# Attention with hashed buckets and a feed-forward block on one core: five kept heads instead of six, GpSimd instructions in column pieces, another order

## The chip, the cores and the metric

The kernel runs on one core of a Trainium2 chip. The metric is the device time in microseconds (us) of one execution; three runs of the kernel before gave a median of 906.74 us. The core's engines are called as in the profile: PE (TensorE, matrix products), DVE (VectorE), ACT (ScalarE), POOL (GpSimd) and SP (SyncE, which issues most DMAs).

## What is computed

Four batches, eight heads, 768 positions, 64 values a head. Queries and keys get a bucket from the signs of six random projections; a position attends only to keys of its own bucket. The attention's output is then put through a feed-forward block with a gelu between two products.

```python
q_bits = (np.einsum('bhsd,dk->bhsk', q, proj) > 0)      # the same for k
mask = q_bucket[:, :, :, None] == k_bucket[:, :, None, :]
scores = np.where(mask, scale * np.matmul(q, k.transpose(0, 1, 3, 2)), -1e9)
attn = exp(scores - max); attn = attn / (attn.sum(-1) + 1e-9)
attn_out = np.matmul(attn, v)                           # (4, 8, 768, 64)
x = attn_out.transpose(0, 2, 1, 3).reshape(3072, 512)
h = x @ w_in                                            # 512 -> 2048
out = (0.5 * h * (1.0 + erf(h / sqrt(2)))) @ w_out      # 2048 -> 512
```

## The kernel before

**Attention.** A unit is 128 query rows of one head against all 768 keys; there are 192 of them. In a unit PE makes the scores (`scores`, L940 in float32, L942 and L943 in half precision), DVE takes the largest of each row out of PSUM (L946), a guard and a shift are worked out for each row (L951 and the helper `affine`, L427 on DVE and POOL, L424 on ACT), ACT takes the exponentials (L960), and DVE the reciprocal of the row sums (L969). Then the probabilities are turned over: for early units by PE transposes (L1019) that DVE or ACT copy out of PSUM into `pt`, later as a rounded half and the rest of it (L427 or L424, and L975) by a DMA transpose. PE multiplies them by the values (L1063 in float32, L1072 in halves).

**Heads.** A head's queries and keys lie in a set of buffers, and the mask is put into extra rows of these. `head_plain` builds a set in float32: two loads, a projection on PE (L893), a sign on ACT, four mask copies. `head` builds it in half precision, each value as a rounded number and a remainder: a load (L588), the largest value on DVE (L591), a scale over all rows (L548 on PE, four small DVE steps), the rounding, three moves of rows, two remainders (L622 on DVE, or on POOL a scaling by L427 and a subtract by L447), a projection (L656), a sign (L662) and four mask copies. Scores of a plain head are two float32 products a unit, of the other heads four half-precision ones.

**Passes.** Batch 0 is worked in two passes over its heads: first 256 query positions (two units a head), then the other 512 (four units a head). Batches 1 to 3 take one pass each. All eight heads of the first pass are plain (`PLAIN = (8, 0)`). Sets with a number below `AGAIN` stay for the second pass, and their heads are used there as they are; the others are built anew by `head`.

**Weights.** The two weight matrices are read as 64-bit words and decoded on DVE (L713, L718, L723), their scale comes from products on PE (L736), and each pair is scaled, rounded and its remainder taken (L427, L424, L447) on ACT, DVE or POOL. This goes on during batch 0. The first product with the output weights waits for all of it.

**Feed-forward.** For each 256 positions PE multiplies by the input weights (L1288), ACT empties PSUM (L1298) and takes the gelu (L1326), the result is split into two halves (L427 or L424, and L1340 on DVE), and PE multiplies by the output weights (L1370). DVE applies the scales (L1400), SP stores.

**Order.** Nothing is ordered by hand. Every step is given to `Plan.add` with a key (what comes first), the steps it needs, a buffer of a ring, and the engines that can do it, each with a cost and an offset. `Plan.order` plays the program through once while it is built: whenever an engine is free, it takes the ready step with the lowest key plus offset. The offsets and many leads in the keys are the numbers in `PAR`, such as `GU_Pool` (the guard on POOL) or `QK1` (scores of the second pass). In that play-through a POOL step and a DVE step marked `port=True` hold a common resource for their whole cost. The result is a fixed order of instructions on each engine. `BLANKS` adds 64 steps of four small products whose results nobody reads, with a late key.

**What the change touches.** `affine` (L419 to L427) and `subtract` (L445 to L447) issue one instruction each for a whole tile. POOL's tiles are up to 1024 columns wide.

Of the kernel before, what the change touches and what calls it, by code (L numbers as in the profile page):

```python
# [16 lines left out]
ALU = mybir.AluOpType  # L17
# [7 lines left out]
FIRST = (((0, 256),), ((256, 256), (512, 256)))  # L25
NEARLY = 2
PLAIN = (8, 0)
AGAIN = 6
BARE = False
WHOLE = (4, 4, 0, 0, 0)  # L30
TABLE = 1.3
# [3 lines left out]
GROW = ("p","hl")  # L35

PAR = dict(
    VB=-40.97, GU_DVE=240.54, GU_Pool=100.45, SH_DVE=167.52, SH_ACT=204, SH_Pool=-19.66, SF_DVE=464.07,
    SF_ACT=-187.68, SF_Pool=-31.21, SU=12.36, NM_DVE=-98.7, NM_ACT=56.76, NM_Pool=-320.58, NM_SP=-162.08,
    NL_DVE=-344.19, NL_Pool=-241.09, XP_ACT=-25.57, XP_DVE=-138.99, NK_DVE=-194.15, NK_ACT=144.23, NK_Pool=21.84,  # L40
    Z=92.38, VS0=-8.93, H0=143.65, HL=-860.3, VS=-892.69, G2=312.6, HQ=577.2, VQ=-429.05, in0=-158.71, out0=424.19,
    in1=-31.4, out1=-40.75, in2=-97.83, out2=-238.27, in3=-146.98, out3=-601.69, H1=-55.7, H2=43.97, H3=-141.96,
    H4=210.7, H5=-617.14, H6=-992.69, H7=-275.83, MEV=-86.92, MGE=-79.83, MSP=-13.76, V0=-31.49, QK0=-585.17,
    QK1=13.9, QK2=-33.94, MX0=267.65, MX1=6.62, MX2=22.49, EX0=-389.34, EX1=-216.58, EX2=102.74, NR0=-69.88,
    NR1=62.63, NR2=328.32, HI0=-23.58, HI1=344.52, HI2=3.95, LO0=119.76, LO1=-21.28, LO2=-1288.81, PV0=-156.22,
    PV1=6.13, PV2=-3.3, TR0=507.72, TR1=-1210.58, TR2=10.73, V1=-212.82, V2=-786.36, Sin0=131.94, Sin1=-52.34,
    Sin2=912.32, Sin3=370.61, Sout0=-163.67, Sout1=81.17, Sout2=33.28, Sout3=700.51, Lin=-140.4, Pin=325.04,
    Qin=957.5, Cin=717.18, Min=-39.13, Lout=-10.95, Pout=-180.7, Qout=-1494.55, Cout=84.08, Mout=-22.24, G0=11.13,
    G1=-61.72, G3=7.9, G4=-238.53, G5=-133.32, G6=227.56, G7=-48.68, DUP0=258.78, DUP1=70.51, DUP2=148.98,
    LOW0=-28.06, LOW1=-108.23, LOW2=151.28, PRJ0=-266.56, PRJ1=451.66, PRJ2=57.45, MSK0=-121.55, MSK1=141.13,  # L50
    MSK2=-103.38, DI_ACT=-220.12, DI_DVE=456.39, DI_Pool=18.53, WS_ACT=839.42, WS_DVE=327.31, WS_Pool=297.28,
    WH_ACT=-283.58, WH_DVE=-111.37, WH_Pool=25.64, WL_ACT=169.18, WL_DVE=120.19, WL_Pool=-197.71, VH_ACT=-176.14,
    VH_DVE=-223.29, VH_Pool=414.86, RND_ACT=472.43, RND_DVE=132.9, RND_Pool=-47.28, HI_ACT=172.21, HI_DVE=-121.04,
    HI_Pool=-46.69, DG_ACT=-163.33, DG_DVE=110.27, DG_Pool=-117.55, EV_ACT=30.92, EV_DVE=1834.91, EV_Pool=-39.8,
    GH_ACT=-198.96, GH_DVE=138.26, GH_Pool=76.2, NS0=116.81, NS1=-68.13, NS2=-261.86,
)
FULL = 65504.0
BIG = 2.0**34
# [18 lines left out]
class Plan:  # L77
# [25 lines left out]
    def add(self, engine, cost, emit, key, needs=(), takes=None, table=None, port=False, act=1.0):  # L103
        s = Step(len(self.steps), engine, cost, emit, key, needs, takes, table, port, act)
        self.steps.append(s)
        return s
# [7 lines left out]
    def free(self, holder, after):  # L114
        hold = {"holder": holder, "left": len(after)}
        for s in after:
            s.frees.append(hold)
# [134 lines left out]
def tile_bucket_attention_moe(  # L252
# [94 lines left out]
    def buf(step):  # L347
# [32 lines left out]
        out=praw[:, NBIT:], in0=praw[:, :NBIT], scalar1=-1.0, scalar2=None, op0=ALU.mult  # L380
# [19 lines left out]
    def add_scale(key, top, t, inv, s, root=False):  # L400
# [17 lines left out]
            top = add("DVE", 0.07, emit, key, [top], port=emit is inverse)  # L418
        return top  # L419

    def affine(engine, out, in_, scale=1.0, bias=0.0):

        if engine == "ACT":
            nc.scalar.activation(out=out, in_=in_, func=AF.Copy, scale=scale, bias=bias)  # L424
        else:
            on = nc.vector if engine == "DVE" else nc.gpsimd
            on.tensor_scalar(out=out, in0=in_, scalar1=scale, scalar2=bias, op0=ALU.mult, op1=ALU.add)  # L427

    def affine_cost(engine, n, pointer=False):
        base, rate, extra = {  # L430
# [13 lines left out]

    def subtract(engine, out, in0, in1):  # L445
        on = nc.vector if engine == "DVE" else nc.gpsimd
        on.tensor_tensor(out=out, in0=in0, in1=in1, op=ALU.subtract)  # L447

    def subtract_cost(engine, n):
        return 0.14 + 1.042e-3 * n if engine == "DVE" else 0.2 + 2.2e-3 * n  # L450
# [4 lines left out]
    def everywhere(t, top, key):  # L455


        def diagonal():
            affine(dg.engine, buf(dg), ident, t[:, 0:1])

        def spread():
            nc.tensor.matmul(buf(pm)[:, :P], ones, buf(dg), start=True, stop=True)

        def biggest():
            nc.vector.tensor_reduce(out=t[:, 1:2], in_=buf(pm)[:, :P], axis=AX.X, op=ALU.max)

        dg = add(affine_on("DI", P, True), 0, diagonal, key, [top], takes="diag", port=True)
        pm = add("PE", 0.11, spread, key, [dg], takes="hp")
        free(dg, [pm])
        sc = add("DVE", 0.2, biggest, key, [pm])  # L470
        free(pm, [sc])
        return sc
# [105 lines left out]
    def head(b, h, i, key, clear, cl):  # L578
# [16 lines left out]
        def high():  # L595
            affine(hi.engine, aq, buf(raw), sc)

        def add_move(dst, src, rd, rs):
            box = []

            def move():
                out, in_ = sets[i][dst][rd], sets[i][src][rs]
                if box[0].engine == "SP":
                    nc.sync.dma_start(out=out, in_=in_)
                else:
                    affine(box[0].engine, out, in_)

            on = {
                "DVE": (0.27, PAR["NM_DVE"]), "ACT": (0.84, PAR["NM_ACT"]), "Pool": (0.9, PAR["NM_Pool"]),
                "SP": (0.45, PAR["NM_SP"]),  # L610
            }
            box.append(add(on, 0, move, key + PAR[f"DUP{cl}"], [hi], port=True))
            return box[0]

        def add_low(dst, rd, rs):
            box = []

            def low():
                out, a = sets[i][dst][rd], aq[rs]
                x = buf(raw)[rs]  # L620
                if box[0].engine == "DVE":
                    nc.vector.scalar_tensor_tensor(  # L622
                        out=out, in0=x, scalar=sc[rs], in1=a, op0=ALU.mult, op1=ALU.subtract
                    )
                else:
                    affine("Pool", x, x, sc[rs])
                    subtract("Pool", out, x, a)

            on = {"DVE": (1.04, PAR["NL_DVE"]), "Pool": (2.8, PAR["NL_Pool"])}
            box.append(add(on, 0, low, key + PAR[f"LOW{cl}"], [hi], port=True))  # L630
            return box[0]
# [160 lines left out]
    def v_scale(b, key):  # L792
# [16 lines left out]
        def load_rows(k):  # L809
            nc.sync.dma_start(  # L810
                out=v_first[:, 2 * k : 2 * k + 2], in_=v[b].rearrange("(c p) d -> p c d", p=P)[:, 2 * k : 2 * k + 2]
            )

        def biggest_rows(k):
            nc.vector.tensor_reduce(
                out=stat_v[:, b, k : k + 1], in_=v_first[:, 2 * k : 2 * k + 2], axis=AX.XY, op=ALU.max,
                apply_absolute_value=True,
            )

        parts = []  # L820
        for k in range(KT // 2 if b == 0 else 0):
            first_v.append(add("SP", 1.8, lambda k=k: load_rows(k), key))
            parts.append(add("DVE", 1.14, lambda k=k: biggest_rows(k), key + PAR["VB"], first_v[-1:]))
        for pr in range(NPAIR if b else 0):
# [10 lines left out]
        if b == 0:  # L835
            key += PAR["VB"]
            early_steps.extend(parts)
# [86 lines left out]
    def unit(t, i, qs, cl, whole, made, place, back):  # L924
# [70 lines left out]
        free(sp, [ex])  # L995
        on = {"DVE": (0.08, PAR["SF_DVE"]), "ACT": (0.23, PAR["SF_ACT"]), "Pool": (0.25, PAR["SF_Pool"])}
        sf = add(on, 0, safe, t - PAR[f"NR{cl}"], [ex])
# [137 lines left out]
    whole = tuple((c, TC) for c in range(0, S, TC))  # L1135
# [26 lines left out]
    for n_pass, (b, chunks) in enumerate(passes):  # L1162
# [7 lines left out]
        for pos, h in enumerate(heads):  # L1170
            pr = h // 2
            if pos % 2 == 0:
                key, mms = t - PAR[f"V{cl}"], []
                whole = pos // 2 < WHOLE[n_pass]
# [6 lines left out]
            i = next((i for i in range(n_sets) if owner.get(i, ())[:2] == (b, h)), None)  # L1181
            kept = i is not None
            if not kept:
                i = min(range(n_sets), key=lambda i: (used.get(i, -1), i))
# [29 lines left out]
        for i in list(owner):  # L1214
            if i >= AGAIN:
                del owner[i]
# [245 lines left out]
```

## Time and profile before

| | |
|---|---|
| three runs | 904.43, 906.74, 910.39 us |
| profiled execution | 905.23 us, span of its instructions 903.4 us |
| granted TensorE clock, mean | 0.991 |
| instructions | 18142 |
| busy ACT | 638.8 us (71%) x1098 |
| first and last product with the input weights (L1288) | 137.7 and 881.4 us |
| first and last product with the output weights (L1370) | 206.7 and 899.4 us |
| last row maximum of a unit (L946) | 725.7 us |

Rows of the profile that name a line and tiles, such as `L427 POOL TENSOR_SCALAR raw<-raw,hs`, give engine, operation, what is written and what is read. In the list of groups the numbers behind the bar are busy us, the mean ns of one instruction, and the idle us of the engine before it with what ended it. In the list of one line's instructions they are minimum, median and maximum in ns, and first and last start in us. In a timeline the first number is the start, the second the duration, both in us, and in brackets stands idle time before it and its releaser. In a table by stretches the stretch is followed by the busy us (and number of instructions) of PE, PE's weight loads, DVE, ACT and POOL, then the granted clock, the DMA share and GB/s. In a list of waits stand the sum in us, the number and the longest.

### The profile page before, as it was taken

Reading aid. Unit: us, or ns where it says so; the run is one execution under the profiler, and the core shown is the slowest. Engines: PE = TensorE matmul, PEld = TensorE weight load, DVE = VectorE, ACT = ScalarE, POOL = GpSimd, SP = SyncE. Lnnn points to the kernel's source line nnn. Section 1 sums busy time; section 2 is a strip of 40 time slices with the busy share of each in tenths; the row PEclk is TensorE's granted clock in tenths of the full one; section 3 lists DMA queues with packets and bytes.
Section 4 is the critical chain, followed back from the end, with each engine's and each line's share of the span. In section 5 each row is a group of like instructions: output and inputs, shape, how many; then the busy total and the mean of one; then the engine's idle time right before and its main releaser. Section 6 shows DMA issues by size and latency. Waiting matters only on the chain.

```text
span 903.4 us, 18142 instructions
## 1 busy us (share of the span) xinstructions
PE 870.2 (96%) x6883; PEld 581.0 (64%) x6883; DVE 686.4 (76%) x1402; ACT 638.8 (71%) x1098; POOL 434.5 (48%) x509
## 2 busy tenths in 40 slices
PE   8999889979999999999999999999999999999998
PEld 5666557756666666676757666757657667676663
DVE  3999989998988799889988998799877861212122
ACT  3687878988888997868998877798877653232221
POOL 2335546667587766766666667666534400000000
PEclk9999989999999999999999999999999999999999
DMA  9962543305597899685968976967767750000000
GB/s 215 241 215 72 146 134 103 106 1 93 97 187 156 163 178 213 123 158 139 174 138 191 190 134 147 177 130 152 134 112 133 134 112 1 24 1 24 1 24 24
DMA packets 281368, 110.67 MB, mean 123 GB/s; under 512 B 228608, under 2 KB 268992, under 8 KB 281280
## 3 DMA queue, kind: packets, MB, share of 16 engines
q1 hardware_dynamic: 280976, 109.51, 57.0%
q8 instruction: 54, 0.88, 0.4%
q14 instruction: 34, 0.28, 0.1%
q10 hardware_dynamic: 304, 0.00, 0.0%
HBM read 42.73 MB, written 6.29 MB: 54 GB/s over the span
## 4 chain that ended last, share of the span: by engine, by line
PE 48%; DVE 8%; ACT 6%; DMA 4%; issue 2%; POOL 1%; SPq 0%; ACTq 0%; POOLq 0%; DVEq 0%
PE hp L1370 19%; PE hp L1288 18%; PE hp L1072 4%; PE s L942 3%; DMA pt<-hl 3%; PE s L943 3%; DVE rows L946 2%; DVE hl L975 2%; ACT p L960 2%; DMA vraw<-v 1%; ACT Q L424 1%; ACT wraw L960 1%; DVE g L1340 1%; DVE wraw L975 1%; ACT hl L424 1%
## 5 line engine op out<-in xcount | busy, mean ns | idle before, releaser
L1288 PE MATMUL hp<-x,Win 128*128 128x256 f16 x2304 | 267.6, 273 | 0.6 <-DVE rows L427 0.3
L1370 PE MATMUL hp<-Wout,g 128*128 128x512 f16 x1152 | 261.5, 379 | 0.0
L1288 PEld LDWEIGHTS <-Win 128*128 128x128 f16 x2304 | 224.3, 98 | 40.2 <-issue 4.0
L1370 PEld LDWEIGHTS <-g 128*128 128x128 f16 x1152 | 110.2, 98 | 127.0 <-issue 5.1
L946 DVE TENSOR_REDUCE rows<-s 128x1 f32<-128x768 f32 x192 | 179.5, 947 | 8.5 <-PE s L943 4.6
L960 ACT ACTIVATE p<-s,rows 128x768 f32<-128x768 f32 x143 | 140.9, 986 | 22.7 <-DVE rows L427 7.7
L1298 ACT ACTIVATE h<-hp,ffs 128x512 f32<-128x512 f32 x96 | 65.3, 681 | 98.4 <-PE hp L1288 98.3
L942 PE MATMUL s<-Q 88*128 88x384 f16 x304 | 99.3, 327 | 8.8 <-ACT p L960 7.2
L427 DVE TENSOR_SCALAR g<-h,ffs 128x512 f16<-128x512 f32 x31 | 15.3, 497 | 111.0 <-ACT h L1326 80.9
L943 PE MATMUL s<-K 128*128 128x384 f16 x304 | 99.2, 326 | 0.0
L427 POOL TENSOR_SCALAR rows<-rows 128x1 f32<-128x1 f32 x111 | 48.6, 437 | 63.9 <-ACT p L960 41.9
L1340 DVE SCALAR_TENSOR_TENSOR g<-h,ffs,g 128x512 f16<-128x512 f32 x96 | 76.1, 806 | 2.8 <-DVE g L427 0.5
L1072 PE MATMUL hp<-pt,vhl 128*64 128x256 f16 x1296 | 76.5, 274 | 0.3 <-ACT h L1298 0.3
L1072 PEld LDWEIGHTS <-vhl 128*64 128x64 f16 x1296 | 68.6, 110 | 10.9 <-issue 10.4
L447 POOL TENSOR_TENSOR K<-raw,Q 64x768 f16<-64x768 f32 x42 | 72.7, 1730 | 3.5
L951 POOL TENSOR_SCALAR rows<-rows,hs 128x1 f32<-128x1 f32 x72 | 47.7, 662 | 51.1 <-DVE rows L946 44.0
L975 DVE SCALAR_TENSOR_TENSOR hl<-p,rows,hl 128x768 f16<-128x768 f32 x54 | 57.7, 1071 | 5.7 <-ACT hl L424 3.0
L960 ACT ACTIVATE wraw<-s,rows 128x768 f32<-128x768 f32 x49 | 48.3, 987 | 7.4 <-POOL rows L427 4.3
L943 PEld LDWEIGHTS <-K 128*128 128x128 f16 x304 | 29.8, 98 | 30.2 <-issue 14.0
L975 DVE SCALAR_TENSOR_TENSOR wraw<-p,rows,wraw 128x768 f16<-128x768 f32 x42 | 45.8, 1090 | 4.1 <-POOL wraw L427 4.0
L427 POOL TENSOR_SCALAR raw<-raw,hs 64x768 f32<-64x768 f32 x42 | 46.0, 1094 | 4.5 <-PE hp L1019 2.2
L940 PE MATMUL s<-K,Q 76*128 76x384 f32 x112 | 44.2, 527 | 3.7 <-ACT p L960 3.5
(163 smaller groups left out, 1371.0 us busy)
## 6 DMA issues: line engine op xcount, KB each, us to landing
raw<-qk SPq DMA_DIRECT2D x26, 384.0 KB, 3.6
vraw<-v SPq DMA_DIRECT2D x24, 384.0 KB, 4.0
wraw<-w_in SPq DMA_DIRECT2D x16, 512.0 KB, 4.6
wraw<-w_out SPq DMA_DIRECT2D x16, 512.0 KB, 4.1
out<-o SPq DMA_DIRECT2D x11, 512.0 KB, 2.8
K<-Q SPq DMA_DIRECT2D x24, 96.0 KB, 2.8
v_first<-v SPq DMA_DIRECT2D x3, 512.0 KB, 11.9
vhl<-v SPq DMA_DIRECT2D x4, 384.0 KB, 7.1
```

The source lines that it names most:

```text
L427: on.tensor_scalar(out=out, in0=in_, scalar1=scale, scalar2=bias, op0=ALU.mult, op1=ALU.add)
L447: on.tensor_tensor(out=out, in0=in0, in1=in1, op=ALU.subtract)
L942: nc.tensor.matmul(to, aq[kk, qs], ak[kk, n], start=True, stop=False)
L943: nc.tensor.matmul(to, bq[:, qs], bk[:, n], start=False, stop=True)
L946: nc.vector.tensor_reduce(out=nm, in_=both(sp), axis=AX.XY, op=ALU.max, negate=True)
L960: nc.scalar.activation(out=buf(ex).rearrange("p (b k) -> p b k", b=2), in_=both(sp), func=AF.Exp, scale=sc, bias=nb, accum_out=ssum,)
L975: nc.vector.scalar_tensor_tensor(out=buf(hi)[:, 1], in0=buf(ex), scalar=r, in1=buf(hi)[:, 0], op0=ALU.mult, op1=ALU.subtract,)
L1072: nc.tensor.matmul(pv[j * D : (j + 1) * D], buf(vh)[:, tv, kt, j * D : (j + 1) * D], buf(holds[j][0])[:, tp * KT + kt, :nt], start=kt == 0 ...
L1288: nc.tensor.matmul(buf(pair[0])[:, j * ch[1] : (j + 1) * ch[1]], win_hl[:, f0 // WB1, tw, pr, f0 % WB1 : f0 % WB1 + P], x[:, tx, pr, : ch[1]],
L1298: nc.scalar.activation(out=values_of()[:, 2 * fp : 2 * fp + 2, :nt], in_=buf(pair[0])[:, : 2 * nt].rearrange("p (j k) -> p j k", j=2), fun ...
L1340: nc.vector.scalar_tensor_tensor(out=gt[:, 1, s2, :nt], in0=h[:, s2, :nt], scalar=sg, in1=gt[:, 0, s2, :nt], op0=ALU.mult, op1=ALU.subtract,)
L1370: nc.tensor.matmul(buf(banks[u]).rearrange("p (c f) -> p c f", c=NWB), gt[:, tg, f, u * P : (u + 1) * P], wout_hl[:, :, tw, ft], start=ft ...
```

## The change

`AGAIN` goes from 6 to 5: five heads of batch 0 stay in float32 for its second pass, and three, not two, are built anew in half precision. `affine` and `subtract` cut a POOL instruction along the first axis behind the partitions when it has more than 512 or 256 elements a partition: 768 columns of a scaling become two instructions of 384, 768 of a subtract three of 256, 1024 two of 512 or four of 256. DVE and ACT instructions stay whole, and the costs that the plan counts with stay as they are. All numbers of `PAR` are other ones, so `Plan.order` gives another order and another division between engines.

```diff
-AGAIN = 6
+AGAIN = 5
...
 PAR = dict(
-    VB=-40.97, GU_DVE=240.54, GU_Pool=100.45, SH_DVE=167.52, SH_ACT=204, SH_Pool=-19.66, SF_DVE=464.07,
-    SF_ACT=-187.68, SF_Pool=-31.21, SU=12.36, NM_DVE=-98.7, NM_ACT=56.76, NM_Pool=-320.58, NM_SP=-162.08,
+    VB=67.25, GU_DVE=142.88, GU_Pool=372.81, SH_DVE=-85.93, SH_ACT=493.57, SH_Pool=68.35, SF_DVE=-887.75,
+    SF_ACT=162.31, SF_Pool=108.68, SU=-62.77, NM_DVE=132.71, NM_ACT=-36.16, NM_Pool=115.43, NM_SP=44.22,
...
+    def pieces(engine, most, *aps):
+
+        whole, n = aps[0].shape[1], 1
+        for size in aps[0].shape[1:]:
+            n *= size
+        count = -(-n // most) if engine == "Pool" else 1
+        cuts = [whole * k // count for k in range(count + 1)]
+        return [tuple(x[:, i:j] for x in aps) for i, j in zip(cuts, cuts[1:])]
...
     def affine(engine, out, in_, scale=1.0, bias=0.0):
...
             on = nc.vector if engine == "DVE" else nc.gpsimd
-            on.tensor_scalar(out=out, in0=in_, scalar1=scale, scalar2=bias, op0=ALU.mult, op1=ALU.add)
+            for o, x in pieces(engine, 512, out, in_):
+                on.tensor_scalar(out=o, in0=x, scalar1=scale, scalar2=bias, op0=ALU.mult, op1=ALU.add)
...
     def subtract(engine, out, in0, in1):
         on = nc.vector if engine == "DVE" else nc.gpsimd
-        on.tensor_tensor(out=out, in0=in0, in1=in1, op=ALU.subtract)
+        for o, x, y in pieces(engine, 256, out, in0, in1):
+            on.tensor_tensor(out=o, in0=x, in1=y, op=ALU.subtract)
```

The prediction speaks of the guard's offsets (`GU_`) and those of the step that adds 1e-9 (`SF_`); the other numbers of `PAR` change in the same way and are left out here.

More of the change, by code (lines that the diff above doesn't have):

```diff
@@ L37 @@
 PAR = dict(
-    VB=-40.97, GU_DVE=240.54, GU_Pool=100.45, SH_DVE=167.52, SH_ACT=204, SH_Pool=-19.66, SF_DVE=464.07,
-    SF_ACT=-187.68, SF_Pool=-31.21, SU=12.36, NM_DVE=-98.7, NM_ACT=56.76, NM_Pool=-320.58, NM_SP=-162.08,
-    NL_DVE=-344.19, NL_Pool=-241.09, XP_ACT=-25.57, XP_DVE=-138.99, NK_DVE=-194.15, NK_ACT=144.23, NK_Pool=21.84,
-    Z=92.38, VS0=-8.93, H0=143.65, HL=-860.3, VS=-892.69, G2=312.6, HQ=577.2, VQ=-429.05, in0=-158.71, out0=424.19,
-    in1=-31.4, out1=-40.75, in2=-97.83, out2=-238.27, in3=-146.98, out3=-601.69, H1=-55.7, H2=43.97, H3=-141.96,
@@ L43 @@
[L43 to L52, printed above, removed]
@@ L53 @@
-    VH_DVE=-223.29, VH_Pool=414.86, RND_ACT=472.43, RND_DVE=132.9, RND_Pool=-47.28, HI_ACT=172.21, HI_DVE=-121.04,
-    HI_Pool=-46.69, DG_ACT=-163.33, DG_DVE=110.27, DG_Pool=-117.55, EV_ACT=30.92, EV_DVE=1834.91, EV_Pool=-39.8,
-    GH_ACT=-198.96, GH_DVE=138.26, GH_Pool=76.2, NS0=116.81, NS1=-68.13, NS2=-261.86,
+    VB=67.25, GU_DVE=142.88, GU_Pool=372.81, SH_DVE=-85.93, SH_ACT=493.57, SH_Pool=68.35, SF_DVE=-887.75,
+    SF_ACT=162.31, SF_Pool=108.68, SU=-62.77, NM_DVE=132.71, NM_ACT=-36.16, NM_Pool=115.43, NM_SP=44.22,
@@ new lines @@
+    NL_DVE=-21.95, NL_Pool=-504.75, XP_ACT=-123.39, XP_DVE=180.18, NK_DVE=-90.24, NK_ACT=-257.23, NK_Pool=-55.95,
+    Z=-107.86, VS0=65.79, H0=-112.84, HL=-846.73, VS=-934.16, G2=389.39, HQ=129.83, VQ=-373.79, in0=-133.17,
+    out0=545.05, in1=-218.36, out1=37.81, in2=194.95, out2=21.39, in3=465.04, out3=52.59, H1=3.14, H2=-183.97,
+    H3=-155.9, H4=131.48, H5=-603.75, H6=-1004.23, H7=-195.76, MEV=266.52, MGE=696.78, MSP=15.46, V0=-120.7,
+    QK0=-118.82, QK1=-287.83, QK2=-180.25, MX0=-320.05, MX1=-49.19, MX2=-219.29, EX0=-612.78, EX1=-167.36,
@@ new lines @@
+    EX2=70.44, NR0=-89.58, NR1=33.83, NR2=-17.38, HI0=-561.14, HI1=248.83, HI2=340.6, LO0=106.64, LO1=-1263.75,
+    LO2=-161.71, PV0=99.03, PV1=115.36, PV2=-77.27, TR0=-1005.23, TR1=-480.94, TR2=45.98, V1=105.26, V2=-194.1,
+    Sin0=149.2, Sin1=64.71, Sin2=7.41, Sin3=246.53, Sout0=-231.58, Sout1=-272.11, Sout2=-372.59, Sout3=194.04,
+    Lin=-157, Pin=341.2, Qin=1120.37, Cin=100.83, Min=-140.12, Lout=-105.73, Pout=458.37, Qout=-2863.3,
+    Cout=-238.38, Mout=162.39, G0=-122.8, G1=-209.72, G3=488.78, G4=20.46, G5=-83.65, G6=-236.82, G7=27.83,
@@ new lines @@
+    DUP0=78.15, DUP1=-85.93, DUP2=-123.07, LOW0=-97.07, LOW1=-66.78, LOW2=18.58, PRJ0=-51.38, PRJ1=841.88,
+    PRJ2=-212.69, MSK0=-114.42, MSK1=426.71, MSK2=228.3, DI_ACT=138.03, DI_DVE=-27.21, DI_Pool=-60.85,
+    WS_ACT=419.32, WS_DVE=65.06, WS_Pool=-21.69, WH_ACT=-803.88, WH_DVE=7.52, WH_Pool=-245.54, WL_ACT=-154.68,
+    WL_DVE=-7.58, WL_Pool=72.47, VH_ACT=-163.46, VH_DVE=-112.9, VH_Pool=63.2, RND_ACT=86.42, RND_DVE=222.34,
+    RND_Pool=221.18, HI_ACT=230.76, HI_DVE=-182.55, HI_Pool=-59.39, DG_ACT=-153.24, DG_DVE=84.64, DG_Pool=151.66,
@@ L56 @@
+    EV_ACT=296.59, EV_DVE=1365.55, EV_Pool=34.42, GH_ACT=-144.99, GH_DVE=2.32, GH_Pool=-76.31, NS0=220.81,
+    NS1=-94.09, NS2=63.07,
 )
```

## The prediction

> **What bounds the kernel now.** I read the page's first part, then the busy times by stage, then what PE (TensorE) waited for.
>
> ```profile
> PE 870.2 (96%) x6883; PEld 581.0 (64%) x6883; DVE 686.4 (76%) x1402; ACT 638.8 (71%) x1098; POOL 434.5 (48%) x509
> ```
>
> ```profile
> 0.00:206.00 206.00, 185.63 (x1393) 125.16 (x1394) 181.87 (x423) 156.06 (x285) 104.14 (x139) 0.96 0.49 136
> 206.00:650.00 444.00, 435.53 (x3643) 289.99 (x3642) 396.19 (x795) 373.81 (x647) 301.94 (x329) 1.00 0.79 155
> 650.00:750.00 100.00, 99.22 (x844) 67.38 (x842) 74.58 (x132) 67.76 (x122) 28.40 (x42) 1.00 0.62 115
> ```
>
> The second fence gives, after the stretch, busy us of PE, PEld, DVE (VectorE), ACT (ScalarE) and POOL (GpSimd). I cut at 206 us because the first matmul against the output weights starts there. Behind it PE has feed-forward work to fill every hole: 435.5 of 444 us are busy, and 99.2 of 100. Ahead of it, PE is busy for 185.6 of 206 and DVE for 181.9: both are nearly full, and PE's 20.4 us of idleness there are 61% of the 33.2 us (903.4 - 870.2) it has in all. So the end moves in two ways: PE gets less work, or PE idles less. What DVE, ACT or POOL save counts only as far as PE was waiting for it.
>
> ```profile
> PE s L942 <- ACT p L960: 7.2, 13, 1.2
> PE hp L1063 <- DVE pt L427: 4.2, 3, 2.2
> PE s L940 <- ACT p L960: 3.9, 5, 1.4
> PE hp L736 <- DVE pt L427: 2.3, 1, 2.3
> ```
>
> PE's longest single waits (2.2, 2.3 us) are for DVE to empty a PSUM bank. They start elsewhere:
>
> ```profile
> 197.65 2.13 POOL L447 TENSOR_TENSOR Wout<-o,Wout 128x1024 f16<-128x1024 f32 x1
> 198.00 0.20 DVE L951 TENSOR_SCALAR rows<-rows,hs 128x1 f32<-128x1 f32 x1
> 198.12 2.21 DVE L427 TENSOR_SCALAR Wout<-o 128x1024 f16<-128x1024 f32 x1
> 198.13 0.19 PEld L1063 LDWEIGHTS hp<-pt,vhl 128*64 128x64 f32 x2 [2.03 <-DVE pt L427]
> 198.13 0.65 PE L1063 MATMUL hp<-pt,vhl 128*64 128x256 f32 x2 [1.80 <-DVE pt L427]
> ```
> ```profile
> 200.37 1.01 DVE L427 TENSOR_SCALAR pt<-hp 128x384 f32<-128x384 f32 x2
> ```
>
> A GpSimd subtract of 1024 columns runs from 197.65 to 199.78. DVE's scaling starts at 198.12 and ends only at 200.33, just after the subtract; behind it stand the two PSUM evictions of 200.37, and PE idles. The reader is to see the chain: long POOL instruction, stretched DVE instruction, late eviction, idle PE. That the stretch is a wait shows in a line whose instruction is always the same size:
>
> ```profile
> L713 DVE TENSOR_SCALAR Wout<-wraw x16: 402/420/2136, 96.2 to 180.7; 128x512 int32<-128x512 int32 x16
> ```
>
> Minimum, median and maximum are 402, 420 and 2136 ns.
>
> **Part 1: the column pieces.** Removed: one long hold of what DVE waits for. Added: more POOL instructions. The price of a cut comes from two widths of each form:
>
> ```profile
> L427 POOL TENSOR_SCALAR raw<-raw,hs x42: 892/907/1689, 90.6 to 648.2; 64x768 f32<-64x768 f32 x42
> ...
> L427 POOL TENSOR_SCALAR g<-h,ffs x18: 687/692/1837, 201.8 to 701.3; 128x512 f16<-128x512 f32 x18
> ...
> L447 POOL TENSOR_TENSOR K<-raw,Q x42: 1633/1640/2224, 92.1 to 649.2; 64x768 f16<-64x768 f32 x42
> ...
> L447 POOL TENSOR_TENSOR Win<-o,Win x8: 2122/2132/2314, 67.9 to 143.4; 128x1024 f16<-128x1024 f32 x8
> ```
>
> Scaling: (907 - 692)/256 = 0.84 ns a column, so 692 - 512 x 0.84 = 0.26 us does not depend on the columns, and each cut adds that. Subtract: (2132 - 1640)/256 = 1.92 ns, 0.17 us a cut; a 256-column piece is an estimated 0.66 us where the whole took 1.64 or 2.13. Fourteen groups of POOL scalings have 768 or 1024 columns, from the 42 above to 2 of the output weights:
>
> ```profile
> L427 POOL TENSOR_SCALAR Wout<-o 128x1024 f16<-128x1024 f32 x2 | 2.4, 1196 | 0.1
> L447 POOL TENSOR_TENSOR Wout<-o,Wout 128x1024 f16<-128x1024 f32 x4 | 9.7, 2430 | 0.4 <-ACT Wout L424 0.2
> ```
>
> They are 162 instructions, one cut each: 162 x 0.26 = 42 us. Subtracts: 42 x 2 cuts and (8 + 4) x 3, so 120 x 0.17 = 20 us. POOL gains 62 us of work; its queue is 48% busy and holds it, but 68% (302 of 444) from 206 to 650, where an estimated 45 of the 62 fall: 78%.
>
> What DVE gets back up to 206: the means of L713 for both weights stand beside its median of 420,
>
> ```profile
> L713 DVE TENSOR_SCALAR Win<-wraw 128x512 int32<-128x512 int32 x16 | 10.9, 686 | 1.1 <-DMA wraw<-w_in 1.1
> ...
> L713 DVE TENSOR_SCALAR Wout<-wraw 128x512 int32<-128x512 int32 x16 | 9.4, 595 | 0.7 <-DMA wraw<-w_out 0.6
> ```
>
> 16 x (0.686 + 0.595 - 2 x 0.42) = 7.1 us for this line. With the 1.7 us from 198.12 to the subtract's end at 199.78 and an estimated 6 for the decoding's other two lines (twice as many instructions as L713) and the rest, I take 15 us of waiting in this stage; a piece leaves a third of a wait on a subtract and some 60% of one on a scaling, so about 9 come back. The stage's DVE is 88% full and PE's waits for evictions above sum to 6.5 us, so I pass half on: **-4.5 us**. Bounds: 0, if PE waits for something else each time, and -9, if all of it counts. Beyond 206 DVE gains as much and POOL loses 45 us, and PE idles for only 8.5 us: I take -0.5, with -4 (half of that idleness) and +10 (the rival below) as bounds.
>
> **Part 2: five heads instead of six.** Head 5 of batch 0 is built a second time, in half precision. PE gives up 4 float32 score units and gets 4 half-precision ones, a projection and one scale:
>
> ```profile
> 157.96 2.85 PE L940 MATMUL s<-rest,x 76*128 76x384 f32 x8
> ```
> ```profile
> 194.80 0.33 PE L942 MATMUL s<-Q 88*128 88x384 f16 x1
> 194.96 0.33 PE L943 MATMUL s<-K 128*128 128x384 f16 x1
> ```
>
> A float32 unit is two calls, which the trace shows as four instructions; so this row is two units, and less the drain of the last one (0.2, an estimate) a unit costs 1.3 us. The half-precision matmuls follow each other every 0.165 us, four a unit: 0.66. So 4 x (1.3 - 0.66) = 2.6 us less, and 0.5 for the projection and 0.2 for the scale more:
>
> ```profile
> 125.10 0.51 PE L656 MATMUL hp<-K,hash 128*32 128x384 f16 x8
> ```
>
> **-1.9 us** of PE. DVE gets a largest-value reduction (0.95 us) and four small ones (an estimated 0.7):
>
> ```profile
> L591 DVE TENSOR_REDUCE tops<-raw 128x1 bf16<-128x768 f32 x26 | 24.6, 946 | 4.0 <-DMA raw<-qk 3.9
> ```
>
> At the same half, +0.8 us. The rounding, two low parts, the row moves and the masks go to whichever of ACT, POOL and DVE is free; if both low parts fall to DVE it is 2 us more, +1 on the path. The extra load (SP queue, one head, 384 KB) goes out well ahead, since set 5 is free after the first pass; if it came late, the head's projection and scores would wait and PE with them, since its order is fixed. Bounds of this part: -2 and +2.
>
> **Part 3: the order.** New offsets mean other neighbours for every instruction. They lean the small row steps towards DVE (guard: POOL 100 to 373, DVE 241 to 143; the 1e-9 step: DVE 464 to -888). A guard costs
>
> ```profile
> L951 DVE TENSOR_SCALAR rows<-rows,hs x80: 184/210/216, 171.7 to 727.5; 128x1 f32<-128x1 f32 x80
> L951 POOL TENSOR_SCALAR rows<-rows,hs x72: 292/710/1563, 175.3 to 720.8; 128x1 f32<-128x1 f32 x72
> ```
>
> 0.21 us on DVE and 0.71 on POOL, so exponentials start earlier and DVE gets up to 72 x 0.21 = 15 us. That PE waits 7.2 + 3.9 us for exponentials says how much there is to win, about 11; DVE's 15 at half say what there is to lose, 7.5. I take -1.5, between them.
>
> Sum: -4.5 - 0.5 - 1.9 + 0.8 - 1.5 = -7.6 us. The profiled execution took 905.2 us (span 903.4 and 1.8 around it), so 897.6. The median of the three runs is 906.7, 1.5 above it; I leave 0.9 for that: **898.5 us**.
>
> **The rivals.**
> *POOL becomes the bound between 206 and 650 (slower).* Its busy time grows by 45 us for cuts, and each of some 200 pieces there can wait for a DVE instruction: the 42 scalings of raw average 1094 ns against a median of 907, 0.19 a time, so 38 us more. 302 + 45 + 38 = 385 of 444, 87%, and some stretches over 100%. From that point guards and masks stand behind pieces, exponentials come late, and PE, whose order is fixed, waits: 1 us more at each of the 13 waits of L942 is +13, and 905.2 + 13 - 1.9 + 1.5 is **918**. For it: POOL guards already take 0.71 instead of 0.29. Against: PE idles 2% there, and lighter DVE makes up part of it.
> *The pieces run into each other and DVE gets nothing back.* Then only the 62 us of POOL and -1.9 remain: +3 on the path, **908**. The Trainium skill (GPSIMD Engine Reference, 2.1 Instruction dispatch) says that a GpSimd core starts the next instruction as soon as its own share of this one is done, and that nothing else holds consecutive instructions apart; by that rule the hold need not end between pieces. Against it stands a case of two POOL instructions back to back:
>
> ```profile
> 644.95 0.90 POOL L427 TENSOR_SCALAR raw<-raw,hs 64x768 f32<-64x768 f32 x1
> ...
> 645.09 1.56 DVE L975 SCALAR_TENSOR_TENSOR hl<-wraw,rows,hl 128x768 f16<-128x768 f32 x1
> ...
> 645.93 2.22 POOL L447 TENSOR_TENSOR K<-raw,Q 64x768 f16<-64x768 f32 x1
> ```
>
> The DVE instruction, stretched to 1.56, ended at 646.65, and the subtract took 2.22 instead of 1.64: DVE got in between the two.
> *The relief is real but PE's waits only change their name*, as PE is at 98% after 206: **905.5**.
> *The order closes most of the early idleness:* three quarters of the 20.4 us (15.3), half of the 8.5 behind it (4.2) and part 2's 1.1: 905.2 - 20.6 + 0.9 = **885.5**. For it: PE also spends 21.1 us on blank matmuls that only keep it running, so the early stage has more room than its idleness tells. Against: DVE, 88% full there, has to do its work in less time.
>
> ```profile
> L392 PE MATMUL hp<-blank 128*128 128x128 bf16 x256 | 21.1, 249 | 3.5 <-DVE both_offs L506 1.9 <-DVE hash L375 1.0 <-ACT pt L424 0.6
> ```
>
> **How the numbers follow.** This kernel's runs tell about 1% from no change, which is 9.1 us of 906.7. Forecast 0.50, of which 0.20 below 897.7 and 0.30 above; POOL bound 0.16, of which 0.14 over 915.8; no gap between pieces 0.06, 0.02 of it over that line; waits renamed 0.10; better order 0.18. Faster by over 1%: 0.20 + 0.18 = 0.38. Slower: 0.14 + 0.02 = 0.16. Within: 0.46. The range runs from 883, just under the better order, to 917, just short of the POOL rival; the forecast's own is 890 to 907.
>
> **What would show it.** Right: L713 and the other stretched DVE lines average near their medians (L713 below 0.5 us); POOL busy rises by 50 to 100 us with some 280 more instructions; L940 has 16 instructions fewer and L591 counts 27; the first output matmul starts 3 to 8 us before 206; PE busy falls by about 2 us plus what the filler matmuls lose. Wrong: the first output matmul no earlier than 206; DVE lines as stretched as before; or PE's idleness between 206 and 650 above 15 us with POOL as the releaser.

## The result and the profile after

Four runs of the changed kernel: 916.18 to 919.17 us, median 916.68, beside 907.47 for the kernel before. The ratio is 1.0107, with a 95% interval of 1.0069 to 1.0146: about 1% slower, where 1% faster was forecast. The profiled execution took 916.96 us, its span is 915.1. Two single executions of other runs below, 1218 and 1471 us at granted clocks of 0.68 and 0.56, are left out of all medians.

The first part of the page of the changed kernel:

```profile
PE 865.3 (95%) x6893; PEld 574.4 (63%) x6893; DVE 677.9 (74%) x1441; ACT 648.7 (71%) x1090; POOL 484.9 (53%) x745
```

PE's busy time is 4.9 us less (865.3 against 870.2), POOL has 236 more instructions and 50 us more. PE is busy for less and done later, so it idles more: 49.8 us, not 33.2. The busy times by stage (changed kernel) say where:

```profile
0.00:206.00 206.00, 187.74 (x1519) 127.32 (x1521) 178.72 (x449) 170.17 (x313) 138.02 (x236) 0.99 0.50 141
206.00:650.00 444.00, 418.97 (x3450) 273.96 (x3446) 382.41 (x786) 365.98 (x610) 312.51 (x456) 1.00 0.76 154
650.00:750.00 100.00, 97.34 (x798) 65.79 (x798) 80.23 (x150) 69.21 (x118) 34.38 (x54) 1.00 0.67 118
```

From 206 to 650 us PE idles for 25.0 us where it idled for 8.5. Up to 206 it idles a little less than before (18.3 against 20.4), but more than the same order with whole instructions, as the first experiment shows. What PE waited for there, in the list of waits of the changed kernel (sum, number, longest):

```profile
PE s L954 <- ACT p L972: 8.6, 18, 1.7
PE hp L668 <- POOL K L459: 6.7, 9, 1.6
PE s L954 <- ACT wraw L972: 4.6, 7, 1.6
```

The second line is new. PE's projection of a head (L656 before, L668 now) waits nine times for POOL's subtract (L447 before, L459 now), the last step of a head's remainder. No such wait stood in the list of the kernel before. One of the nine, first on POOL and DVE, then on PE (timelines of the changed kernel):

```profile
634.70 2.95 POOL L438 TENSOR_SCALAR raw<-raw,hs 64x384 f32<-64x384 f32 x2
...
635.34 1.01 DVE L987 SCALAR_TENSOR_TENSOR hl<-p,rows,hl 128x768 f16<-128x768 f32 x1
636.26 1.01 DVE L987 SCALAR_TENSOR_TENSOR wraw<-wraw,rows,wraw 128x768 f16<-128x768 f32 x1
...
637.73 1.93 POOL L459 TENSOR_TENSOR K<-raw,Q 64x256 f16<-64x256 f32 x3
```
```profile
635.74 1.47 PE L1300 MATMUL hp<-x,Win 128*128 128x256 f16 x12
637.14 0.34 PE L668 MATMUL hp<-K,hash 128*32 128x384 f16 x1
639.08 0.34 PE L668 MATMUL hp<-K,hash 128*32 128x384 f16 x2 [1.60 <-POOL K L459]
```

The scaling's two pieces and the subtract's three take 4.96 us from 634.70 to 639.66. Two pieces of a scaling have a median of 0.59 us each, so 2.95 holds some 1.8 us of waiting: two DVE instructions run from 635.34 to 637.27, and the scaling ends 0.4 us after them. So a cut has two prices in this case, its own and the chance that DVE gets in. PE issues in its fixed order, so nothing that stands behind the projection can fill the 1.6 us.

The first product with the output weights, which was to start some us before 206, starts at 208.6 (L1370 before, L1382 in the changed kernel's list by line):

```profile
L1382 PE MATMUL hp<-Wout,g x1152: 376/379/390, 208.6 to 910.9; 128*128 128x512 f16 x192
```

So the early stage won nothing against the kernel before.

### The profile page after: what moved, and what is told of

Same layout as the page of the kernel before. It is cut to its first block, busy times and chain, and to the rows that moved or that the text cites. A ratio compares the mean times of both kernels' runs of the same rounds, so it can differ in the third digit from the quotient of the medians.

```text
span 915.1 us, 18464 instructions
## 1 busy us (share of the span) xinstructions
PE 865.3 (95%) x6893; PEld 574.4 (63%) x6893; DVE 677.9 (74%) x1441; ACT 648.7 (71%) x1090; POOL 484.9 (53%) x745
## 5 line engine op out<-in xcount | busy, mean ns | idle before, releaser
L1382 PE MATMUL hp<-Wout,g 128*128 128x512 f16 x1152 | 261.6, 379 | 0.0
L1382 PEld LDWEIGHTS <-g 128*128 128x128 f16 x1152 | 109.9, 98 | 126.3 <-issue 4.4
L459 POOL TENSOR_TENSOR K<-raw,Q 64x256 f16<-64x256 f32 x120 | 93.5, 805 | 3.2
L987 DVE SCALAR_TENSOR_TENSOR hl<-p,rows,hl 128x768 f16<-128x768 f32 x66 | 72.2, 1096 | 13.4 <-POOL hl L438 11.2
L963 POOL TENSOR_SCALAR rows<-rows,hs 128x1 f32<-128x1 f32 x67 | 45.1, 674 | 57.5 <-DVE rows L958 52.8
L438 POOL TENSOR_SCALAR raw<-raw,hs 64x384 f32<-64x384 f32 x82 | 55.0, 675 | 20.3 <-ACT Q L434 8.2
L955 PEld LDWEIGHTS <-K 128*128 128x128 f16 x304 | 29.8, 98 | 37.6 <-issue 21.6
L438 DVE TENSOR_SCALAR rows<-rows 128x1 f32<-128x1 f32 x163 | 28.3, 179 | 29.6 <-ACT p L972 21.2
L438 POOL TENSOR_SCALAR hl<-p,rows 128x384 f16<-128x384 f32 x50 | 33.0, 672 | 30.0 <-DMA pt<-hl 20.8
```

Of the source, the lines that this page charges most:

```text
L438: on.tensor_scalar(out=o, in0=x, scalar1=scale, scalar2=bias, op0=ALU.mult, op1=ALU.add)
L459: on.tensor_tensor(out=o, in0=x, in1=y, op=ALU.subtract)
L955: nc.tensor.matmul(to, bq[:, qs], bk[:, n], start=False, stop=True)
L987: nc.vector.scalar_tensor_tensor(out=buf(hi)[:, 1], in0=buf(ex), scalar=r, in1=buf(hi)[:, 0], op0=ALU.mult, op1=ALU.subtract,)
L1382: nc.tensor.matmul(buf(banks[u]).rearrange("p (c f) -> p c f", c=NWB), gt[:, tg, f, u * P : (u + 1) * P], wout_hl[:, :, tw, ft], start=ft ...
```

## The experiments

Times are medians, with the kernel before run beside them on the same chip (medians of 907.5 to 909.1 us).

**First: pieces, order and number of kept heads taken apart.**

Whole instructions, order and five heads of the change (`whole_new_order`; no engine is called "none", so nothing is cut):

```diff
-        count = -(-n // most) if engine == "Pool" else 1
+        count = -(-n // most) if engine == "none" else 1
```

> The changed kernel with POOL's instructions whole again; five kept heads and the new order stay. Theory P (the pieces cost: they lengthen POOL's part of building a head between 206 and 650 us, and PE waits for it): 905 to 910 us, the 6.7 us in which PE's projections waited for POOL's subtract fall below 2 us, and PE's idleness from 206 to 650 us falls from 25 to about 12. Theory O (the order costs: the new offsets place work worse, the pieces are nearly free): 914 to 919 us, with PE's idleness there still above 20. Theory R (the pieces help, and the order is worse than it looks): above 919, with DVE lines stretched as in the kernel before.

Measured: **892.8 us**, ratio 0.9841 (0.9800 to 0.9881). Faster than either kernel, and 24 us below the changed one. That is the side of theory P, but 12 us below its range: the order was worth more than any theory gave it. Run again later on another chip (`whole_again`): 895.3, ratio 0.9869 (0.9836 to 0.9903).

> The changed kernel's order with whole instructions once more, on the same chip as the three runs beside it: 890 to 896 us by all theories. It is what they are compared with.

The page and the stage from 206 us of the first of the two:

```profile
PE 863.5 (97%) x6893; PEld 575.9 (65%) x6893; DVE 674.5 (76%) x1441; ACT 647.4 (73%) x1090; POOL 401.9 (45%) x482
```
```profile
206.00:650.00 444.00, 433.91 (x3662) 288.61 (x3660) 393.65 (x814) 379.70 (x636) 268.52 (x310) 1.00 0.79 159
```

PE idles for 10.1 us there, against 25.0 with pieces. Its list of waits holds no projection that waits for POOL, and shorter waits for exponentials:

```profile
PE s L954 <- ACT p L972: 6.4, 14, 0.9
...
PE s L954 <- ACT wraw L972: 1.8, 3, 0.8
```

The pieces cost POOL 83 us (484.9 - 401.9). DVE's busy time, which holds its waits, was to fall with them; it is 674.5 whole (676.2 in `whole_again`) and 677.9 in pieces. Up to 206 us PE idles for 13.8 us whole (15.3 in `whole_again`) and 18.3 in pieces.

Pieces on the kernel before (`pieces_old_order`): the two helpers of the change put into it, with `AGAIN = 6` and the old `PAR`.

> The kernel before with POOL's instructions in pieces and nothing else changed: six kept heads, old order. Theory P: 914 to 920 us, with PE idle for 20 us or more between 206 and 650 us instead of 8.5. Theory O: 904 to 909 us. Theory R: 898 to 903 us, as DVE's long waits up to 206 us shrink and the first output product starts some us before 206.

Measured: 932.6 us, ratio 1.0278 (1.0245 to 1.0310), 12.6 us above theory P's range. The pieces cost 24 to 26 us in either order, which is theory P's direction and more than its size. Theories O and R are out as accounts of the total. The stages, the first product with the output weights and the wait for the subtract in this run:

```profile
0.00:206.00 206.00, 187.52 (x1433) 126.30 (x1434) 179.29 (x433) 160.62 (x294) 127.11 (x219) 0.98 0.49 136
206.00:650.00 444.00, 415.11 (x3396) 271.26 (x3395) 371.41 (x742) 347.33 (x602) 336.10 (x491) 0.98 0.76 147
```
```profile
L1381 PE MATMUL hp<-Wout,g x1152: 376/379/634, 201.1 to 926.2; 128*128 128x512 f16 x192
```
```profile
PE hp L667 <- POOL K L458: 5.1, 6, 1.8
```

In this order the early relief is there, as theory R had it: the first product with the output weights starts at 201.1 us instead of 206.7, and PE idles for 18.5 us up to 206 instead of 20.4. From 206 to 650 it idles for 28.9 instead of 8.5, and the projection waits for POOL here too.

Five kept heads with the old numbers (`five_old_numbers`: `-AGAIN = 6`, `+AGAIN = 5` alone), and the new numbers with six (`six_new_numbers`: the new `PAR` alone):

> The kernel before with five kept heads instead of six, all offsets and whole instructions as before; the plan works out its order anew from that. Theory P and theory R: within 5 us of 907, since PE loses 2 us and DVE gains as much, and an order that is not fitted to it may cost a little. Theory O, in the form that rebuilding a third head is what disturbs: 912 us or more, with the wait in the stretch of batch 0's second pass, 100 to 210 us.

> The kernel before with the new offsets alone: six kept heads, whole instructions. Theory P: 903 to 910 us. Theory O: 914 us or more, with PE idle above 20 us between 206 and 650 us. Theory R: 916 us or more, with DVE stretched as before. The order here is not the changed kernel's own, since the plan sees one head less to build; it tells of the offsets in general.

Measured: 929.9 us, ratio 1.0235 (1.0197 to 1.0273), and 911.4 us, ratio 1.0027 (1.0002 to 1.0052). Neither half of the change's other part is a gain by itself; together they are 12 to 14 us faster. Each set of numbers goes with its own count of heads. `six_new_numbers` lies 1.4 us above theory P's range. `five_old_numbers` lies where theory O put it, 18 us above the range of theories P and R, and is disturbed late in the stretch that it named and right behind it. Two stages of the kernel before, then of this run:

```profile
150.00:206.00 56.00, 50.02 (x408) 35.05 (x407) 53.24 (x129) 49.90 (x89) 38.12 (x36) 0.97 0.27 76
206.00:250.00 44.00, 43.11 (x334) 29.13 (x334) 40.80 (x89) 36.81 (x65) 28.50 (x32) 1.00 0.58 107
```
```profile
150.00:206.00 56.00, 45.15 (x306) 29.97 (x305) 49.60 (x131) 48.91 (x88) 37.09 (x33) 0.79 0.18 50
206.00:250.00 44.00, 35.98 (x284) 25.36 (x282) 38.74 (x78) 37.17 (x64) 29.53 (x30) 0.92 0.63 124
```

PE idles for 18.9 us from 150 to 250 instead of 6.9, which is 12.0 of the 20.6 us that it idles more in all, and the granted clock there is lower. The first product with the output weights starts at 244.8 us. How much of the 12 to 14 us is due to the third rebuilt head and how much to the order can't be told apart.

**Second: which pieces, and whether it is their number or their size.** The base is the changed order with all whole, 892.8 us.

`subtracts_in_pieces` and `scalings_in_pieces` cut one kind only:

```diff
-            for o, x in pieces(engine, 512, out, in_):
+            for o, x in pieces("whole", 512, out, in_):
```
```diff
-        for o, x, y in pieces(engine, 256, out, in0, in1):
+        for o, x, y in pieces("whole", 256, out, in0, in1):
```

> The changed kernel with only the subtracts in pieces, scalings whole. All of this call stand against 892.8 us with everything whole and 916.7 with everything in pieces, in the same order. Theory F (what costs is the fixed price of each cut, which makes POOL late in an order worked out without it): the scalings' cuts are about two thirds of the added POOL time (162 x 0.27 us against 120 x 0.18), so subtracts alone give a third of the 24 us: 898 to 904 us. Theory L (what costs is that at each boundary a DVE instruction gets in and the rest of the POOL tile waits for it): the subtracts have most of the waits by DVE and build the heads that PE waited for: 908 to 915 us.

> The changed kernel with only the scalings in pieces, subtracts whole. Theory F: two thirds of the 24 us, 905 to 912 us. Theory L: 896 to 903 us. If the two kinds together give much more or much less than 24 us over the whole ones, they act through one another.

Measured: 899.3 us (ratio 0.9912, 0.9878 to 0.9946) and 898.5 (0.9899, 0.9864 to 0.9934). They cost 6.5 and 5.7 us; both together cost 24. Neither theory foresaw that they are far from adding up; the expectation of the second run names it as a sign that the kinds act through one another.

`weights_in_pieces` cuts only tiles of 1024 columns:

```diff
-        count = -(-n // most) if engine == "Pool" else 1
+        count = -(-n // most) if engine == "Pool" and n == 1024 else 1
```

> The changed kernel with pieces only for tiles of 1024 columns, that is for the weights up to about 206 us; all of attention's and the heads' POOL instructions whole. Theory F and theory L: no cuts where POOL delays PE, so 890 to 896 us. If the relief of DVE is worth what the prediction gave it (4.5 us), most of it comes from these tiles: 886 to 890 us. If it is above 897, cuts cost in the early stage too.

Measured: 896.9 us, ratio 0.9869 (0.9832 to 0.9907), the same ratio as `whole_again` and 4.1 and 1.6 us above the two whole runs. The relief of DVE in the early stage, the prediction's -4.5 us, is not there in this order.

`uneven_pieces` keeps the number of pieces but gives nearly all columns to the last (the subtracts of the input weights stay in four even ones):

```diff
-        cuts = [whole * k // count for k in range(count + 1)]
+        cuts = [k * max(1, whole // 384) for k in range(count)] + [whole]
```

> The changed kernel with as many pieces as it has, but uneven: all pieces but the last have 2 columns (64 in tiles of the weights that are split by blocks; the subtracts of the input weights stay in four even pieces), the last has all the rest. POOL pays the fixed price of each cut, and DVE's longest wait is as long as with whole instructions. Theory F: 915 to 925 us, as much as the even pieces or more, since the relief is gone. Theory L: 896 to 906 us, since a boundary right behind a piece of 2 columns seldom finds a DVE instruction waiting.

Measured: 917.3 us, ratio 1.0109 (1.0059 to 1.0159), as the changed kernel. Its page:

```profile
PE 867.5 (95%) x6893; PEld 575.6 (63%) x6893; DVE 687.5 (75%) x1441; ACT 649.9 (71%) x1090; POOL 476.1 (52%) x745
```

DVE is busy for 687.5 us against 677.9 with even pieces: long holds cost it 9.6 us of waiting, and the end moves by 0.6 us, less than the runs can tell (the interval is about 4.5 us to either side). So the time lies in theory F's range and not in theory L's, and 9.6 us of DVE's waiting show nothing at the end. What theory L describes is not excluded by it: DVE gets in behind the narrow pieces too. The 2-column scaling of a remainder averages 454 ns, with a minimum of 253.

**Third: why one kind costs little and both cost much.**

`counted_pieces` tells the plan of the price and keeps the pieces; `counted_whole` has the same order and whole instructions:

```diff
+        if engine == "Pool":
+            base += 0.27 * (-(-n // 512) - 1)
         return base + rate * n + extra * pointer
...
-        return 0.14 + 1.042e-3 * n if engine == "DVE" else 0.2 + 2.2e-3 * n
+        return 0.14 + 1.042e-3 * n if engine == "DVE" else 0.2 + 2.2e-3 * n + 0.18 * (-(-n // 256) - 1)
...
-            on = {"DVE": (1.04, PAR["NL_DVE"]), "Pool": (2.8, PAR["NL_Pool"])}
+            on = {"DVE": (1.04, PAR["NL_DVE"]), "Pool": (3.43, PAR["NL_Pool"])}
```

(The move of a head's rows on POOL likewise goes from 0.9 to 1.17.)

> The changed kernel, with the plan told of the cuts' price: its costs of POOL steps grow by 0.27 us for each cut of a scaling and 0.18 for each of a subtract (a remainder of a head on POOL 3.43 instead of 2.8). Five heads, the same offsets, pieces as in the change; the plan gives another order from these costs. To be read against the next run, which has this order and whole instructions. Theory U (the price hurts because the order was worked out without it): less than 12 us above the next run, instead of 24. Theory T (POOL time hurts as such): 20 us or more above it. The order itself is one that no offset was fitted to, so its level may be anything from 890 to 930 us.

> The order of the run before, worked out with the cuts' price, and whole instructions. Theory U: at most 12 us below the run before, and any level from 890 to 925 us. Theory T: 20 us or more below it.

Measured: 912.8 us, ratio 1.0060 (1.0032 to 1.0088), and 915.4, ratio 1.0066 (1.0038 to 1.0094). In this order the pieces cost nothing that the runs can tell, although POOL is 48 us busier from 206 to 650 (first line with pieces, second whole):

```profile
206.00:650.00 444.00, 424.10 (x3508) 278.12 (x3506) 383.70 (x805) 374.01 (x626) 307.99 (x445) 0.98 0.79 153
```
```profile
206.00:650.00 444.00, 422.45 (x3516) 277.92 (x3513) 385.98 (x803) 373.38 (x625) 259.70 (x277) 0.98 0.77 153
```

POOL time as such (theory T) is out. That the price hurts because the order was worked out without it (theory U) fits, but is not shown alone: this order is slow by itself, and PE idles from 206 to 650 us for 19.9 us with pieces and 21.6 with whole instructions, where the order of the change has 10.1. An order that waits elsewhere anyway may hide the pieces as well. An order's level over 910 may come from numbers fitted to other costs; that too is not shown.

`heads_in_pieces` cuts only in the building of half-precision heads, `all_but_heads_in_pieces` everywhere else. The helpers get a parameter `cut`; shown are the calls of the first run, which the second has with `cut=False`:

```diff
+            affine(hi.engine, aq, buf(raw), sc, cut=True)
...
+                    affine(box[0].engine, out, in_, cut=True)
...
+                    affine("Pool", x, x, sc[rs], cut=True)
+                    subtract("Pool", out, x, a, cut=True)
```

> The changed kernel with pieces only where a head is built in half precision (rounding, moves of rows, remainders), whole instructions for weights, probabilities and values. Against 892.8 us with all whole and 916.7 with all in pieces. Theory H (the chain that builds a head is what PE waits for): 908 to 916 us. Theory Q (POOL has slack, which any cuts use up, and only what is beyond it counts): about half of the 62 us of cuts, so 896 to 904 us.

> The other half: pieces for weights, probabilities and values, whole instructions where a head is built. Theory H: 892 to 898 us. Theory Q: 895 to 903 us; both halves then add up to clearly less than the 24 us of all pieces.

Measured: 908.9 us, ratio 1.0002 (0.9970 to 1.0034), and 896.3, ratio 0.9888 (0.9829 to 0.9948). Against the two whole runs the heads cost 14 to 16 us and the rest 1 to 4, both as theory H had it. The two halves do not add up to the 24 of all pieces.

The last three cut only the remainders of heads on POOL (41 of them): both kinds as in the change, the subtract alone in three, the subtract alone in six. The helpers get a parameter `most`, the widest piece; shown are the calls of the first run. The other two have `most=4096` for the scaling, that is whole, and 256 or 128 for the subtract.

```diff
-                    affine("Pool", x, x, sc[rs])
-                    subtract("Pool", out, x, a)
+                    affine("Pool", x, x, sc[rs], most=512)
+                    subtract("Pool", out, x, a, most=256)
```

> The changed kernel with pieces only in the remainders of a head on POOL: scaling in two, subtract in three; everything else whole. One remainder takes 2 x 0.59 + 3 x 0.67 = 3.19 us where the plan counts with 2.8. Theory M (the order has a margin: a remainder may grow from 2.55 to about 2.8, and PE waits for what is beyond): 904 to 911 us, as heads in pieces. Theory S (the heads' other cuts, rounding and moves of rows, take part as much): 896 to 902 us.

> Pieces only in the remainders' subtracts, three each: 0.91 + 3 x 0.67 = 2.92 us, just past the plan's 2.8. Theory M: 892 to 898 us. Theory S: about the same, 893 to 899.

> Pieces only in the remainders' subtracts, six of 128 columns: an estimated 0.91 + 1.64 + 5 x 0.18 = 3.45 us, past the plan's 2.8 by more than both cuts of the change together, though the scalings are whole. Theory M: 908 us or more. If it is a property of cutting both kinds, and not the length: 894 to 902 us.

The scaling and the subtract of a remainder, from the lists by line (minimum/median/maximum in ns), of `whole_again`, `remainder_both`, `remainder_subtract_3` and `remainder_subtract_6`:

```profile
L438 POOL TENSOR_SCALAR raw<-raw,hs x41: 894/910/1691, 59.1 to 634.9; 64x768 f32<-64x768 f32 x41
...
L459 POOL TENSOR_TENSOR K<-raw,Q x40: 1635/1642/2227, 89.5 to 635.9; 64x768 f16<-64x768 f32 x40
```
```profile
L438 POOL TENSOR_SCALAR raw<-raw,hs x82: 572/588/1367, 58.9 to 650.3; 64x384 f32<-64x384 f32 x82
...
L459 POOL TENSOR_TENSOR K<-raw,Q x120: 663/669/1437, 90.2 to 652.2; 64x256 f16<-64x256 f32 x120
```
```profile
L459 POOL TENSOR_TENSOR K<-raw,Q x120: 661/669/1457, 88.0 to 640.2; 64x256 f16<-64x256 f32 x120
```
```profile
L459 POOL TENSOR_TENSOR K<-raw,Q x240: 418/426/1206, 88.5 to 662.1; 64x128 f16<-64x128 f32 x120
```

These medians leave out what a piece waits for DVE. The means hold it (lists of groups of `whole_again`, then of `remainder_both`):

```profile
L459 POOL TENSOR_TENSOR K<-raw,Q 64x768 f16<-64x768 f32 x40 | 68.7, 1717 | 3.3
L438 POOL TENSOR_SCALAR raw<-raw,hs 64x768 f32<-64x768 f32 x41 | 45.3, 1104 | 19.8 <-ACT Q L434 7.7 <-DVE Q L438 6.2 <-issue 3.2
```
```profile
L459 POOL TENSOR_TENSOR K<-raw,Q 64x256 f16<-64x256 f32 x120 | 90.8, 782 | 3.2
L438 POOL TENSOR_SCALAR raw<-raw,hs 64x384 f32<-64x384 f32 x82 | 56.4, 692 | 21.3 <-ACT Q L434 8.1 <-DVE Q L438 6.3 <-issue 2.4
```

The table has the length of one remainder from the medians and from the means, and beside it what was measured; PE's idleness is 444 less its busy time from 206 to 650 us, and the last column is PE's wait of L668 for POOL's subtract:

| run | medians, us | means, us | time, us | ratio (interval) | PE idle 206-650 | L668 waits |
|---|---|---|---|---|---|---|
| `whole_again` | 0.91 + 1.64 = 2.55 | 2.82 | 895.3 | 0.9869 (0.9836-0.9903) | 10.1 | none |
| `remainder_subtract_3` | 0.91 + 3 x 0.67 = 2.92 | 3.37 | 900.7 | 0.9926 (0.9889-0.9964) | 15.1 | 1.3 |
| `remainder_both` | 2 x 0.59 + 3 x 0.67 = 3.18 | 3.73 | 909.0 | 1.0005 (0.9977-1.0034) | 19.6 | 4.4 |
| `remainder_subtract_6` | 0.91 + 6 x 0.43 = 3.47 | 4.18 | 917.6 | 1.0107 (1.0058-1.0155) | 23.3 | 7.3 |

The rows behind the last two columns of the longest:

```profile
206.00:650.00 444.00, 420.73 (x3472) 275.60 (x3469) 382.37 (x785) 367.32 (x614) 294.10 (x459) 0.99 0.77 154
```
```profile
PE hp L668 <- POOL K L459: 7.3, 7, 2.1
```

The remainders alone cost as much as all cuts in the heads (909.0 beside 908.9), so rounding and moves of rows take no part that the runs can tell: theory M, and not S. Six pieces of the subtract with a whole scaling cost more than both cuts of a remainder, so it is the remainder's length and not which kinds are cut. Scalings alone make 2.82 us by the medians and subtracts alone 2.92, which fits the small cost of one kind.

By the means the length grows by 0.55, 0.91 and 1.36 us, of which the cuts' own price is 0.37, 0.63 and 0.92. About a third is waiting for DVE, which gets in between pieces; theory L has that share in the length.

Theory M holds in its main point. Whether the price starts at the plan's 2.8 us is open. Its 892 to 898 for three pieces was too low, but the interval of the measured 900.7 runs from 898.4 to 905.2, and by the means a whole remainder takes 2.82 already, which would leave no margin.

No experiment delayed the remainders by something other than cuts, and the level of an order fitted anew to the true costs wasn't tried.

## Why the prediction was wrong, step by step

**What bounds the kernel.** Right: PE, with its idleness as what moves the end. Wrong was the step from it: "PE idles for only 8.5 us", used as if little idleness behind 206 us meant little to lose there. Little idleness bounds a gain, not a loss. In the same order PE went from 10.1 to 25.0 us of idleness there when POOL's times changed.

**Part 1, the price of a cut.** The 0.26 and 0.17 us were right (2 x 588 - 907 = 269 ns; (3 x 669 - 1640)/2 = 184 ns). The 62 us of POOL became 83 between the two kernels of the same order, with 263 cuts instead of 282. The rest fits more waiting for DVE: the pieces of remainders average 675 and 805 ns in the changed kernel, against medians of 588 and 669. The prediction's sum has no term for waits that a cut adds; only its first rival does.

**Part 1, the path.** This is the step that failed: "Beyond 206 ... I take -0.5, with -4 (half of that idleness) and +10 (the rival below) as bounds". Measured, pieces cost 24 us, so the term was put near nothing where it is the largest of all. What was missing is the path from a remainder to PE, though the text knew that the order is fixed: a remainder grew from 2.55 to 3.18 us by the medians (2.82 to 3.77 with its waits), the projection waited 6.7 us for it with all of PE behind it, and cuts in the remainders alone cost 13.7 us (909.0 - 895.3). The plan's costs, which stayed as they were, are a likely reason that the order had no room for it; that is argued and not shown. Which waits make up the rest of the 24 us stays open: PE idles 21.5 us more in all (49.8 against 28.3), 4.5 of them up to 206 us.

**Part 1, the relief.** The chain at 198 us was read rightly, and "half" of 9 us was put on the path. In the order that it was read from, part of it came: with pieces the first product with the output weights starts 5.6 us earlier (`pieces_old_order`), 4.9 us before 206 where the prediction's sign has 3 to 8, and PE idles 1.9 us less up to 206. In the order of the change it did not come: 207.2 and 210.0 us in the two whole runs, 208.6 in pieces, and PE idles more. There was also less to win. In `whole_new_order` (list of groups) L725, the line that averaged 686 and 595 ns before, takes

```profile
L725 DVE TENSOR_SCALAR Wout<-wraw 128x512 int32<-128x512 int32 x16 | 7.8, 487 | 0.9 <-DMA wraw<-w_out 0.6
L725 DVE TENSOR_SCALAR Win<-wraw 128x512 int32<-128x512 int32 x16 | 6.8, 431 | 0.4 <-DMA wraw<-w_in 0.4
```

In `whole_again` it takes 588 and 471, in the changed kernel 518 and 434. So the sign at which the prediction said it would be right (L713 below 0.5 us) came true on average, but one of the two whole runs shows it as well. Two of its signs of being wrong came true: the first product with the output weights no earlier than 206 us, and PE's idleness between 206 and 650 above 15 us, with POOL as the releaser of the new wait.

**Parts 2 and 3, five heads and the order.** -1.9 + 0.8 - 1.5 = -2.6 us were predicted, measured are -14.5 (908.9 x (1 - 0.9841)) and -11.9 in the second run: the right sign, a fifth of the size. The "better order" rival, 885 us, was nearer for this part.

**The rivals.** The POOL rival gave 918, and the slower side came with nearly its time, but not by its mechanism: POOL is busy for 312.5 of 444 us (70%), not 87, and no stretch had to be full. Its sentence that "PE, whose order is fixed, waits" holds; it put the wait at the exponentials, where 8.6 + 4.6 us stand against 6.4 + 1.8 in the same order with whole instructions, and missed the projection. That pieces run into each other is not what happened: DVE waits 9.6 us less with even than with uneven pieces, and in the timeline at 634.70 two DVE instructions run while the second piece of a scaling waits, so DVE gets in between them. By the Trainium skill (GPSIMD Engine Reference, 2.1 Instruction dispatch) a GpSimd core goes on to the next instruction when its own share is done. The hold ends between pieces all the same, as these rows show. Counted from the kernel before, the pieces were put at -5.0 us and measured at +24, and parts 2 and 3 at -2.6 and measured at -14.5: two large terms of opposite sign, of which +9.5 is left. That the kernel came out only 1% slower is luck of that sum and no sign that the terms were nearly right.

## What to carry to other kernels

Where the order of instructions is fixed, a longer instruction on an engine with time to spare can cost more than it seems to: what counts is whether the engine that waits in order stands behind it. Here one chain of two instructions, 41 times in the kernel, gave over half of the loss. Telling the plan the new cost made the pieces free and the whole kernel no faster, so the costs and the numbers that were fitted to them would have to be found together. A full engine's small idleness says how little can be won there, not how little can be lost. Before an engine's stall is cut, give the same instructions their cost without the benefit (uneven pieces): it tells in one run what the stall was worth at the end, as long as the instructions' other waits stay alike.

## What was not expected of the hardware

Cutting what DVE waits for did not always lower the sum of its waits. Its busy time, which includes them, is 674.5 and 676.2 us in the change's order with whole instructions and 677.9 in pieces. In the order of the kernel before it fell from 686.4 to 681.5 (`pieces_old_order`), and from 685.2 in `counted_whole` to 677.7 in `counted_pieces`. In the change's order the longest waits get shorter, but there are more of them. Against the fastest tenth of their kind, 45 DVE instructions in the trace of `whole_new_order` are stretched by over 0.15 us, the longest by 1.8; in that of the changed kernel it is 75, the longest by 0.56. With as many cuts and long last pieces DVE is busy for 687.5 us, so shorter holds are worth 9.6 us to DVE at an equal number of instructions.

POOL pays for it: in the changed kernel a remainder takes 3.77 us on average, where its pieces add up to 3.18 by the medians; whole it is 2.82 against 2.55.
